# A two-layer cached-attention decode step: caches laid out with 64 consecutive keys in a partition, V loaded in pairs of slots

## The chip, the cores and the metric

The kernel runs on one core of a Trainium2 chip. The metric is device microseconds of one execution, lower is better. The core has five engines with a queue each: PE (TensorE, matrix products; its weight loads are a row of their own, PEld), DVE (VectorE), ACT (ScalarE), POOL (GpSimd) and SP (SyncE, which here only issues transfers). Sixteen DMA engines move data between the chip's main memory and the on-chip buffer of 128 partitions.

## The reference

One decode step for 8 batch rows, through an attention block A and an MLP block B, twice, with the same weights and the same caches both times. Everything is bfloat16.

```python
B, Sq, D = 8, 1, 512
Hq, Hkv, Sk, Dh = 32, 8, 8192, 128
...
q = (x @ wq)                      # 32 query heads of 128
k, v = repeat(k_cache, 4), repeat(v_cache, 4)      # 4 query heads share one cached head
p = softmax(q . k * Dh ** -0.5)
o = (p . v) @ wo
...
x = x + A(layernorm(x)); x = x + silu(layernorm(x) @ w1) @ w2
x = x + A(layernorm(x)); x = x + silu(layernorm(x) @ w1) @ w2
```

K and V hold 8 rows x 8 heads x 8192 keys x 128 values each, 128 MiB apiece. For one row and head that is 2 MiB of K and 2 MiB of V. Since a softmax and the sum over its keys don't depend on the order of the keys, any order will do as long as K and V agree on it.

## The kernel before

**Tasks.** A task is one layer, one batch row and one cached head (128 tasks). `make_tasks` (L141) writes out their order by hand. Heads 0, 1 and 2 of each row, and half of head 3, have their K loaded in both layers; the last 18 granules of K of each row (half of head 3, and heads 4 to 7) are *kept*: loaded for layer 0 and left in the buffer until layer 1 of the same row. For each row the order is: layer 0 of the heads 3 to 7 ("kept heads, first pass"), then five or six tasks that fill the time (heads 0 to 2 of other rows, of either layer), then layer 1 of heads 3 to 7 (little K to load, V only). The next row's first pass follows directly. While the filling tasks run, the row's own chain (output projection, LayerNorm, MLP, LayerNorm, query projection of layer 1) is worked off in small stages between them, since layer 1 needs its query.

**Granules, groups and slots.** A task's 8192 keys are four granules of 2048 keys (512 KB of K and of V), and each granule is two groups of 1024 keys. `ARENA` (L248) is 27 slots of one granule, 4 KB in each partition. In a granule, partition p holds 16 consecutive keys, and a granule is one solid 512 KB piece of memory (L354).

**Order of the loads.** `plan_loads` (L172) lists every load with the group before which it is needed and the group after which its slot is free again: a K granule is needed LT = 2 groups before its first group's scores and free after its second group's; a V granule is needed, and freed, LP = 12 groups behind its scores. The list is sorted by need, and each load takes the slot that comes free earliest. `issue` (L352) sends one load on SP, which first waits until the slot's last readers are done; `issue_until(p)` (L394) sends, after group p has been emitted, those at the head of the list whose slot is free by the plan. The list is never overtaken. At the start the first four K granules go out, then wq, then all loads into untouched slots, then wo, w1 and w2 (`load_rest`, L401).

**A group's work.** The main loop (L748) steps through the groups p, 1024 keys each:

- `emit_t` (L424): eight 128x128 transposes of K on PE into PSUM (L433), and a copy of 128x1024 back over the slot (by DVE, L441, or ACT, L439); kept K in layer 1 is already transposed.
- `emit_s` (L458): the scores of a granule, four matmuls of 512 columns (L464).
- the softmax of the task before, spread over the eight steps of the next (the table `soft`, L735): at step 0 the row maximum and a spread of it along the diagonal (`softmax_max`, `spread`, L475 and L477); at step 1 a matmul with a matrix of ones that hands it to all partitions (L485), the shift (`own`, `shift`, L488 and L491) and the exponential into `P` (ACT, L495); at step 3 the sums (L501, and on POOL L504); at step 4 the transposes of P (L513) and their copy to `PT` (L517); at step 7 the reciprocal (L524).
- `emit_pv` (L526): P times V, 12 groups behind the scores, 16 matmuls for a granule (L537), and at the task's end `emit_norm` (L542).

Buffers: two `PT`, separate `spread` and `own`, four sets of sums (NST = 4), a 128x128 matrix `ones`, a `far` of 64 columns (four equal copies of 16), and separate buffers for the LayerNorm (`xc`, `sq`, `xnT`, `vr`) and the MLP (`eh`, `hsT`). `op` (L320) adds the waits: an instruction waits for the last writer of what it reads, and for the readers of what it writes.

Of the kernel before, what the change touches and what calls it, by code (L numbers as in the profile page):

```python
# [5 lines left out]
HQ = 32  # L6
DH = 128
SM_SCALE = DH ** -0.5
LN_EPS = 1e-5
# [6 lines left out]
NSLOT = 27  # L16
KEEP = 18
LT = 2
PRE = 10
LP = 12  # L20
# [4 lines left out]
NPT = 2  # L25
NQB = 2
NST = 4
# [102 lines left out]
class Load:  # L130


    __slots__ = ("kind", "b", "g", "k", "need", "free", "slot", "after")

    def __init__(self, kind, b, g, k, need, free):
        self.kind, self.b, self.g, self.k = kind, b, g, k
        self.need, self.free = need, free
        self.slot, self.after = None, None
# [32 lines left out]

def plan_loads(tasks, kept, nslot, ngran):  # L172

    at = {t: i for i, t in enumerate(tasks)}
    loads = []
    for i, (layer, b, g) in enumerate(tasks):
        for k in range(ngran):
            i0 = i * GPT + k * GPG
            if layer == 0 or (g, k) not in kept:
                need = -1 if i0 < PRE else i0 - LT  # L180
                last = i if layer or (g, k) not in kept else at[(1, b, g)]
                loads.append(Load("K", b, g, k, need, last * GPT + (k + 1) * GPG - 1))
            loads.append(Load("V", b, g, k, i0 + GPG - 1 + LP, i0 + GPG - 1 + LP))
    loads.sort(key=lambda d: (d.need, d.kind))
    free = [(-2, s) for s in range(nslot)]
    for d in loads:
        free.sort()
        d.after, d.slot = free.pop(0)
        assert d.after < d.need or d.need == -1 and d.after == -2, (d.kind, d.need, d.after)
        free.append((d.free, d.slot))  # L190
    return loads
# [18 lines left out]
def _build(ctx, nc, A_x, A_k_cache, A_v_cache, A_wq, A_wo, B_w1, B_w2, out):  # L210
# [59 lines left out]
    QB = [sb([128, NGRAN - 1 + QUAD], BF16, "QB") for _ in range(NQB)]  # L270
    at1 = [sb([128, HQ], BF16, "at1") for _ in range(3)]
    at2 = sb([128, HQ, B], BF16, "at2")
    vr = sb([128, B], FP32, "vr")
    yr = sb([128, B], FP32, "yr")
    tr = sb([128, B], FP32, "tr")
    s1 = sb([128, B], FP32, "s1")
    s1a = sb([128, B], FP32, "s1a")
    xc = sb([128, KT, B], FP32, "xc")
    sq = sb([128, KT, B], FP32, "sq")
    xnT = sb([128, KT, B], BF16, "xnT")  # L280
    eh = sb([128, FT * B], FP32, "eh")
    hsT = sb([128, FT * B], BF16, "hsT")
# [3 lines left out]
    PT = [sb([128, CPB, NQ * USED], BF16, "PT") for _ in range(NPT)]  # L286
    ones = sb([128, 128], FP32, "ones")
    hm = sb([128, REP], FP32, "hm")
    real = sb([128, 1], FP32, "real")
    far = sb([128, NQ * USED], FP32, "far")  # L290
    rowmax = sb([128, 1], FP32, "rowmax")
    spread = sb([128, NQ * USED], FP32, "spread")
    own = sb([128, NQ * USED], FP32, "own")
    shift = sb([128, 1], FP32, "shift")
    rs = [sb([128, 1], FP32, "rs") for _ in range(NST)]
    ssm = [sb([128, REP], FP32, "ssm") for _ in range(NST)]
    ssa = [sb([128, REP], FP32, "ssa") for _ in range(NST)]
    rcp = [sb([128, REP], FP32, "rcp") for _ in range(NST)]

# [52 lines left out]
    def issue(d):  # L352
        cache = A_k_cache if d.kind == "K" else A_v_cache
        src = cache[d.b, d.g].rearrange("(k p c) d -> k p (c d)", k=NGRAN, p=128)[d.k]  # L354
        dst = ARENA[:, d.slot * SLOT:(d.slot + 1) * SLOT]
        dma(sp, dst, src, slsem[d.slot], writes=[r_half(d.slot, 0), r_half(d.slot, 1)])
        (k_slot if d.kind == "K" else v_slot)[(d.b, d.g, d.k)] = d.slot

    with nc.Block() as block:

        @block.sync
        def _(sync_eng):
# [11 lines left out]
            op(dve, lambda: dve.memset(ones[:, :], 1.0), writes=["ones"])  # L374
            for n in range(NQB):
                op(pool, lambda n=n: pool.memset(QB[n][:, :], 0.0), writes=[f"QB{n}"])
# [4 lines left out]
                    hm[:, :], lanes.rearrange("p c (r k) -> p r c k", k=NGRAN), AX.XY, ALU.add),  # L381
                reads=["ident"], writes=["hm"],
            )
            op(dve, lambda: dve.tensor_reduce(real[:, :], hm[:, :], AX.X, ALU.add), reads=["hm"], writes=["real"])
            for c in range(NQ):
                op(dve, lambda c=c: dve.tensor_scalar(
                    far[:, c * USED:(c + 1) * USED].rearrange("p (r k) -> p r k", k=NGRAN),
                    hm[:, :].unsqueeze(2).to_broadcast([128, REP, NGRAN]), real[:, 0:1], -FAR,
                    op0=ALU.subtract, op1=ALU.mult),
                   reads=["hm", "real"], writes=["far"])  # L390
# [15 lines left out]
            for _n in range(NGRAN):  # L406
                issue(queue.pop(0))
# [65 lines left out]
            def softmax_max(ti):  # L473
                bank = ti % NSCP
                op(dve, lambda: dve.tensor_reduce(rowmax[:, :], SCp[bank][:, :], AX.X, ALU.max),  # L475
                   reads=[f"SC{bank}"], writes=["rowmax"])
                op(dve, lambda: dve.tensor_scalar(  # L477
                    spread[:, :].rearrange("p (c q) -> p c q", q=USED), lanes, rowmax[:, 0:1], -SM_SCALE,
                    op0=ALU.mult, op1=ALU.mult),
                   reads=["ident", "rowmax"], writes=["spread"])  # L480

            def softmax_shift(ti):
                ob = ti % 2
                every = OTp[ob][:, 0:NQ * USED]
                mm_group([lambda: pe.matmul(every, ones[:, :], spread[:, :], start=True, stop=True)],  # L485
                         reads=["ones", "spread"], writes=[f"OT{ob}"])

                op(dve, lambda: dve.scalar_tensor_tensor(  # L488
                    own[:, :], every, real[:, 0:1], far[:, :], op0=ALU.mult, op1=ALU.add),
                   reads=[f"OT{ob}", "real", "far"], writes=["own"])  # L490
                op(dve, lambda: dve.tensor_reduce(shift[:, :], own[:, :], AX.X, ALU.min), reads=["own"], writes=["shift"])  # L491

            def softmax_exp(ti):
                bank, st = ti % NSCP, ti % NST
                op(act, lambda: act.activation(  # L495
                    P[:, :], SCp[bank][:, :], ACT.Exp, bias=shift[:, 0:1], scale=SM_SCALE, accum_out=rs[st][:, :]),
                   reads=[f"SC{bank}", "shift"], writes=["P", f"rs{st}"])

            def softmax_sum(ti):
                st = ti % NST  # L500
                op(dve, lambda: dve.tensor_scalar(  # L501
                    ssm[st][:, :], hm[:, :], rs[st][:, 0:1], None, op0=ALU.mult),
                   reads=["hm", f"rs{st}"], writes=[f"ssm{st}"])
                op(pool, lambda: pool.partition_all_reduce(ssa[st][:, :], ssm[st][:, :], 128, bass.bass_isa.ReduceOp.add),  # L504
                   reads=[f"ssm{st}"], writes=[f"ssa{st}"])

            def emit_pt(ti):
                pb = ti % NPT
# [9 lines left out]
                    PT[pb][:, :, :].rearrange("p x (c q) -> p x c q", q=USED),  # L518
                    tpv.rearrange("p x (c q) -> p x c q", q=QUAD)[:, :, :, 0:USED]),
                   reads=[f"TP{tb}"], writes=[f"PT{pb}"])  # L520

            def softmax_rcp(ti):
                st = ti % NST
                op(dve, lambda: dve.reciprocal(rcp[st][:, :], ssa[st][:, :]), reads=[f"ssa{st}"], writes=[f"rcp{st}"])  # L524

            def emit_pv(i):  # L526
# [3 lines left out]
                ob, pb = ti % 2, ti % NPT  # L530
                pv = PT[pb][:, :, :].rearrange("p x (c r k) -> p x c k r", c=NQ, k=NGRAN)
# [10 lines left out]
                mm_group(steps, reads=[r_half(slot, h), f"PT{pb}"], writes=[f"OT{ob}"])  # L542

            def emit_norm(ti):
# [6 lines left out]
                op(dve, lambda: dve.tensor_tensor(dst, OTp[ob][:, 0:REP * PVN:PVN], rcp[st][:, :], ALU.mult),  # L551
                   reads=[f"OT{ob}", f"rcp{st}"], writes=[rd])

            def ln_stages(xv, rx, n):

                xcv, sqv, xnv = xc[:, :, 0:n], sq[:, :, 0:n], xnT[:, :, 0:n]
# [7 lines left out]
                def second():  # L564
# [6 lines left out]
                        reads=["s1a", rx], writes=["xc"],  # L571
                    )
                    op(dve, lambda: dve.tensor_tensor(sqv, xcv, xcv, ALU.mult), reads=["xc"], writes=["sq"])
                    op(dve, lambda: dve.tensor_reduce(s1[:, 0:n], sqv.rearrange("p k b -> p b k"), AX.X, ALU.add),
                       reads=["sq"], writes=["s1"])
                    op(pool, lambda: pool.partition_all_reduce(s1a[:, 0:n], s1[:, 0:n], 128, bass.bass_isa.ReduceOp.add),
                       reads=["s1"], writes=["s1a"])
                def third():
                    v, y = vr[:, 0:n], yr[:, 0:n]
                    vi, yi = v.bitcast(INT32), y.bitcast(INT32)  # L580
                    op(dve, lambda: dve.tensor_scalar(v, s1a[:, 0:n], 1.0 / D, LN_EPS, op0=ALU.mult, op1=ALU.add),
                       reads=["s1a"], writes=["vr"])
                    op(dve, lambda: dve.tensor_scalar(yi, vi, 1, None, op0=ALU.logical_shift_right),
                       reads=["vr"], writes=["yr"])
# [4 lines left out]
                def newton(rounds):  # L589
                    v, y, t = vr[:, 0:n], yr[:, 0:n], tr[:, 0:n]  # L590
                    for _n in range(rounds):
                        op(dve, lambda: dve.tensor_tensor(t, y, y, ALU.mult), reads=["yr"], writes=["tr"])
                        op(dve, lambda: dve.scalar_tensor_tensor(t, t, -0.5, v, op0=ALU.mult, op1=ALU.mult),  # L593
                           reads=["tr", "vr"], writes=["tr"])
# [3 lines left out]
                def fourth():  # L598
# [3 lines left out]
                       reads=["xc", "yr"], writes=["xnT"])  # L602
# [51 lines left out]
            def block_stages(xs, rxs, n, fine=False):  # L654
# [4 lines left out]

                def expo():  # L660
                    op(act, lambda: act.activation(eh[:, 0:FT * n], MISC[:, 0:FT * n], ACT.Exp, scale=-1.0),
                       reads=["MISC"], writes=["eh"])

                def silu():
                    ev = eh[:, 0:FT * n]
                    op(dve, lambda: dve.tensor_scalar(ev, ev, 1.0, None, op0=ALU.add), reads=["eh"], writes=["eh"])
                    op(dve, lambda: dve.reciprocal(ev, ev), reads=["eh"], writes=["eh"])
                    op(dve, lambda: dve.tensor_tensor(hsT[:, 0:FT * n], MISC[:, 0:FT * n], ev, ALU.mult),
# [169 lines left out]
```

## Time and profile before

| | |
|---|---|
| time, median of 3 runs | 1208.69 us (1207.76 to 1209.6) |
| profiled execution: span from first to last instruction | 1205.7 us |
| bytes read from memory | 473.44 MB, 393 GB/s over the span |
| K loads, V loads | 368 and 512, 512 KB each |
| transposes of K on PE (L433) | 5888, 418.5 us busy |
| P times V on PE (L537) | 8192, 296.0 us busy |
| copies of transposed K: DVE (L441), ACT (L439) | 317.1 us, 278.7 us busy |
| mean granted TensorE clock | 0.977 |

The profile is of one execution, and its span is 3.0 us under the median of the three runs. Its rows give an engine's busy time, its share of the span and the count of its instructions. The rows in 40 slices show how the busy share, the clock and the transfer rate run over the span. "DMA packets" are the single pieces that the DMA engines move, counted by size. A group's idle time names what ended it, so a PE that waits for K shows it as released by the transfer. A window's line gives each engine's busy time in that stretch, the granted PE clock, the mean busy share of the 16 DMA engines (packets overlap, so it can be a little over 1), and GB/s.

### The profile page before, as it was taken

What the parts mean: (1) busy time and instruction counts of PE and PEld (TensorE: products, weight loads), DVE (VectorE), ACT (ScalarE), POOL (GpSimd) and SP (SyncE); (2) the same over time, 40 slices, a digit from 0 to 9 for tenths busy, and PEclk for the clock granted to TensorE, in tenths of its full rate; (3) what the DMA queues carried; (4) which work ended last, traced back from release to release, by engine and by line L of the source; (5) the groups of instructions that cost most, each with busy time, mean ns of one, the idle gap of its engine ahead of it and who ended that gap; (6) DMA issues with size and microseconds to landing.
All of it is one profiled execution on the core that took longest, in us unless ns stands there. A gap on an engine that the chain in (4) does not pass through costs nothing.

```text
span 1205.7 us, 45853 instructions
## 1 busy us (share of the span) xinstructions
PE 981.2 (81%) x20216; PEld 772.2 (64%) x20216; DVE 611.8 (51%) x1853; ACT 386.1 (32%) x670; POOL 70.8 (6%) x172
## 2 busy tenths in 40 slices
PE   2868898778888788878888898788888898889885
PEld 2656675667666676667666676667666675667564
DVE  2534564446445554546454554446454554456443
ACT  1323332333233332333233332333233333333231
POOL 0000000000000000000000000000000000000000
PEclk7889999999999999999999999999999999999996
DMA  9999999999999999999999999999999999999994
GB/s 370 385 398 408 403 405 406 408 406 399 396 408 408 408 371 404 408 407 403 399 408 407 405 378 408 409 407 395 385 408 407 401 402 407 408 404 398 390 408 172
DMA packets 133926, 476.43 MB, mean 395 GB/s; under 512 B 14160, under 2 KB 20064, under 8 KB 133216
## 3 DMA queue, kind: packets, MB, share of 16 engines
q1 hardware_dynamic: 133728, 473.51, 99.6%
q8 instruction: 159, 2.61, 0.9%
q14 instruction: 39, 0.32, 0.1%
HBM read 473.44 MB, written 0.01 MB: 393 GB/s over the span
## 4 chain that ended last, share of the span: by engine, by line
DMA 47%; PE 32%; DVE 11%; issue 5%; SPq 3%; ACT 2%; POOL 0%; POOLq 0%; ACTq 0%; DVEq 0%
DMA arena<-in_A_k_cache_dram 45%; PE TPp L433 9%; PE OTp L537 9%; PE SCp L464 5%; PE MISC L613 5%; DVE arena L441 3%; SPq L334 3%; DMA arena<-in_A_v_cache_dram 2%; ACT P L495 2%; PE OTp L485 2%; PE TPp L513 1%; DVE rowmax L475 1%; DVE PT L517 1%; PE MISC L631 1%; DVE tr L593 1%
## 5 line engine op out<-in xcount | busy, mean ns | idle before, releaser
L441 DVE COPY arena<-TPp 128x1024 bf16<-128x1024 bf16 x460 | 317.1, 690 | 384.0 <-PE TPp L433 383.6
L433 PE MATMUL TPp<-ident,arena 128*128 128x128 bf16 x5888 | 418.5, 221 | 110.4 <-DMA arena<-in_A_k_cache_dram 92.0
L433 PEld LDWEIGHTS TPp<-ident,arena 128*128 128x128 bf16 x5888 | 341.3, 99 | 129.7 <-DMA arena<-in_A_k_cache_dram 108.9
L439 ACT COPY arena<-TPp 128x1024 bf16<-128x1024 bf16 x276 | 278.7, 1010 | 395.5 <-PE TPp L433 395.4
L537 PEld LDWEIGHTS OTp<-PT,arena 128*128 128x128 bf16 x8192 | 243.1, 96 | 158.7 <-issue 104.5
L537 PE MATMUL OTp<-PT,arena 128*128 128x48 bf16 x8192 | 296.0, 184 | 33.3 <-DVE at L551 9.6
L464 PE MATMUL SCp<-arena,QB 128*32 128x512 bf16 x2048 | 206.8, 394 | 4.9 <-issue 2.1
L495 ACT ACTIVATE P<-SCp,shift 128x512 bf16<-128x512 f32 x128 | 88.0, 687 | 381.7 <-DVE shift L491 261.9
L504 POOL PARTITION_ALL_REDUCE ssa<-ssm x128 | 56.2, 439 | 940.8 <-DVE ssm L501 923.4
L475 DVE TENSOR_REDUCE rowmax<-SCp 128x1 f32<-128x512 f32 x128 | 87.5, 684 | 33.8 <-PE SCp L464 33.8
L464 PEld LDWEIGHTS SCp<-arena,QB 128*32 128x32 bf16 x2048 | 52.9, 93 | 53.0 <-issue 3.3
L485 PE MATMUL OTp<-spread,ones 128*128 128x64 f32 x256 | 55.2, 297 | 28.4 <-DVE spread L477 27.1
L513 PE MATMUL TPp<-ident,P 128*128 128x128 bf16 x512 | 50.0, 220 | 21.9 <-ACT P L495 20.2
L488 DVE SCALAR_TENSOR_TENSOR own<-OTp,real,far 128x64 f32<-128x64 f32 x128 | 36.3, 284 | 53.4 <-PE OTp L485 53.2
L485 PEld LDWEIGHTS OTp<-spread,ones 128*128 128x128 f32 x256 | 38.6, 190 | 36.9 <-DVE spread L477 35.5
L501 DVE TENSOR_SCALAR ssm<-hm,rs 128x4 f32<-128x4 f32 x128 | 28.8, 225 | 42.8 <-ACT P L495 42.8
L513 PEld LDWEIGHTS TPp<-ident,P 128*128 128x128 bf16 x512 | 32.0, 98 | 26.8 <-ACT P L495 23.8
L613 PE MATMUL MISC<-xnT,wq 128*128 128x32 bf16 (+1 forms) x1152 | 38.7, 176 | 4.2 <-issue 2.8
L517 DVE COPY PT<-TPp 128x256 bf16<-128x256 bf16 x128 | 36.4, 285 | 9.6 <-PE TPp L513 9.6
L631 PE MATMUL MISC<-at,wo 128*128 128x32 bf16 (+1 forms) x1152 | 39.9, 175 | 0.3 <-DVE at L551 0.3
L613 PEld LDWEIGHTS MISC<-xnT,wq 128*128 128x128 bf16 x1152 | 35.0, 96 | 5.3 <-issue 3.2
L631 PEld LDWEIGHTS MISC<-at,wo 128*128 128x128 bf16 x1152 | 35.3, 97 | 0.4 <-DVE at L551 0.4
(47 smaller groups left out, 296.3 us busy)
## 6 DMA issues: line engine op xcount, KB each, us to landing
arena<-in_A_v_cache_dram SPq DMA_DIRECT2D x512, 512.0 KB, 10.7
arena<-in_A_k_cache_dram SPq DMA_DIRECT2D x368, 512.0 KB, 15.1
wq<-in_A_wq_dram SPq DMA_DIRECT2D x1, 4096.0 KB, 16.3
wo<-in_A_wo_dram SPq DMA_DIRECT2D x1, 4096.0 KB, 26.5
w<-in_B_w_dram SPq DMA_DIRECT2D x2, 1792.0 KB, 23.1
P<-in_A_x_dram SPq DMA_DIRECT2D x1, 8.0 KB
out_dram<-P SPq DMA_DIRECT2D x1, 8.0 KB
```

The costliest lines, as they stand in the source:

```text
L433: lambda c=c: pe.transpose(tpv[:, c, :], chunk(slot, h * GRP + c), ident[:, :])
L439: op(act, lambda: act.copy(dst, TPp[tb][:, :]), reads=[f"TP{tb}"], writes=[r_half(slot, h)])
L441: op(dve, lambda: dve.tensor_copy(dst, TPp[tb][:, :]), reads=[f"TP{tb}"], writes=[r_half(slot, h)])
L464: lambda c=c: pe.matmul(SCp[bank][c * QUAD:(c + 1) * QUAD, :], QB[qn][:, NGRAN - 1 - k:NGRAN - 1 - k + QUAD], ARENA[:, slot * SLOT + c * K ...
L475: op(dve, lambda: dve.tensor_reduce(rowmax[:, :], SCp[bank][:, :], AX.X, ALU.max), reads=[f"SC{bank}"], writes=["rowmax"])
L485: mm_group([lambda: pe.matmul(every, ones[:, :], spread[:, :], start=True, stop=True)], reads=["ones", "spread"], writes=[f"OT{ob}"])
L495: op(act, lambda: act.activation(P[:, :], SCp[bank][:, :], ACT.Exp, bias=shift[:, 0:1], scale=SM_SCALE, accum_out=rs[st][:, :]), reads=[f" ...
L504: op(pool, lambda: pool.partition_all_reduce(ssa[st][:, :], ssm[st][:, :], 128, bass.bass_isa.ReduceOp.add), reads=[f"ssm{st}"], writes=[f ...
L513: lambda c=c: pe.transpose(tpv[:, c, :], P[:, c * 128:(c + 1) * 128], ident[:, :])
L537: lambda c=c, cc=cc: pe.matmul(otp, chunk(slot, h * GRP + c), pv[:, cc % CPB, cc // CPB % NQ, k, :].unsqueeze(2).to_broadcast([128, REP, P ...
L613: lambda o=o, k=k: pe.matmul(MISC[:, o * n:o * n + w], w_sb[:, k, o * 128:(o + 1) * 128], rhs_of(k).to_broadcast([128, w]) if n == 1 else ...
L631: lambda o=o, h=h: pe.matmul(MISC[:, o * w:(o + 1) * w], wo_sb[:, h, o * 128:(o + 1) * 128], rhs_of(h).to_broadcast([128, w]) if n == 1 el ...
```

## The change

**Layout.** A head's 8192 keys are now split over the partitions first: partition p holds keys 64p to 64p+63, 16 KB that lie together in memory. Granule k is the k-th quarter of that in every partition, 4 KB, and granules k and k+1 of a partition are one run of 8 KB.

**Wider loads.** A load may cover several granules that go to neighbouring slots: two for V (VWIDE), all the kept granules of a head for K (four, or two for head 3), one for other K (KWIDE). Only the semaphore of the first of its slots counts it. A wide load is needed when its first granule is, and it can go out when the last of its slots is free.

**Plan.** There are 28 slots. The upper 18 are homes, a fixed place for each kept granule; the other 10 are for streaming. Other loads may use a home too, if they are done with it at least AHEAD = 10 us before the kept head needs it. The plan keeps a clock (PACE: 1.24 us a group, 0.64 us where K is already there). For each load, in order of need, it takes the slot or run of slots with the longest lead (capped at ENOUGH = 14 us), then the least idle waiting of one slot for another, then the one that came free last. A load of two or four whose lead would be under EARLIEST (7 or 14 us) is split in halves.

**Small buffers.** To make room for the slot: one `PT`; `spread` and `own` lie in P's bytes, as do the MLP's buffers for all rows at once, while the LayerNorm's for all rows lie in PT's; two sets of sums; `ones` is a column that is repeated by the access pattern, `far` 16 columns repeated likewise; the rest are columns of one tensor `small`, and the chain's `xc`, `sq` and `eh` share columns and one name for the waits; `vr` is written over `s1a`.

```diff
-NSLOT = 27
+NSLOT = 28
...
+KWIDE = 1
+VWIDE = 2
+EARLIEST = {1: 0.0, 2: 7.0, 4: 14.0}
+ENOUGH = 14.0
+AHEAD = 10.0
+PACE = (1.24, 0.64)
...
-NPT = 2
-NST = 4
+NST = 2
...
 def plan_loads(tasks, kept, nslot, ngran):
...
+        if kind == "K":
+            need = -1 if i0 < PRE else i0 - LT
+            end = i if home is None else at[(1, b, g)]
+            free = [end * GPT + (k + 1) * GPG - 1 for k in ks]
+        else:
+            need = i0 + GPG - 1 + LP
+            free = [i * GPT + (k + 1) * GPG - 1 + LP for k in ks]
+        heapq.heappush(heap, (need, kind, i, ks, Load(kind, i, b, g, ks, need, free, home)))
...
+            for slot in range(nslot - n + 1):
+                held = free[slot:slot + n]
+                if any(r and lead(r[0], f) < AHEAD for r, f in zip(reserved[slot:slot + n], d.free)):
+                    continue
+                after = max(held)
+                waste = sum(clock[max(0, after)] - clock[max(0, f)] for f in held)
+                key = (-min(lead(d.need, after), ENOUGH), waste, -after, slot)
+                best = key if best is None else min(best, key)
+            if n > 1 and (best is None or -best[0] < EARLIEST[n]):
+                push(d.kind, d.task, d.ks[:n // 2])
+                push(d.kind, d.task, d.ks[n // 2:])
+                continue
+            d.slot = best[-1]
+        d.after = max(free[d.slot:d.slot + n])
...
-    PT = [sb([128, CPB, NQ * USED], BF16, "PT") for _ in range(NPT)]
-    ones = sb([128, 128], FP32, "ones")
+    PTb = sb([128, CPB * NQ * USED], BF16, "PT")
+    Pf = P[:, :].bitcast(FP32)
+    spread = Pf[:, 0:NQ * USED]
+    own = Pf[:, NQ * USED:2 * NQ * USED]
...
     def issue(d):
         cache = A_k_cache if d.kind == "K" else A_v_cache
-        src = cache[d.b, d.g].rearrange("(k p c) d -> k p (c d)", k=NGRAN, p=128)[d.k]
-        dst = ARENA[:, d.slot * SLOT:(d.slot + 1) * SLOT]
+        n = len(d.ks)
+        rows = cache[d.b, d.g].rearrange("(p c) d -> p (c d)", p=128)
+        src = rows[:, d.ks[0] * SLOT:(d.ks[0] + n) * SLOT]
+        dst = ARENA[:, d.slot * SLOT:(d.slot + n) * SLOT]
...
-            for _n in range(NGRAN):
+            while len(k_slot) < NGRAN:
                 issue(queue.pop(0))
...
-                mm_group([lambda: pe.matmul(every, ones[:, :], spread[:, :], start=True, stop=True)],
-                         reads=["ones", "spread"], writes=[f"OT{ob}"])
+                mm_group([lambda: pe.matmul(every, ones.to_broadcast([128, 128]), spread, start=True, stop=True)],
+                         reads=["ones", "P"], writes=[f"OT{ob}"])
```

## The prediction

> **What bounds the kernel now.** I read the page from the top (span, engines, slices, queues), then windows of the DMA rate, then what the PE waits for. First the page:
>
> ```profile
> span 1205.7 us, 45853 instructions
> PE 981.2 (81%) x20216; PEld 772.2 (64%) x20216; DVE 611.8 (51%) x1853; ACT 386.1 (32%) x670; POOL 70.8 (6%) x172
> ...
> GB/s 370 385 398 408 403 405 406 408 406 399 396 408 408 408 371 404 408 407 403 399 408 407 405 378 408 409 407 395 385 408 407 401 402 407 408 404 398 390 408 172
> DMA packets 133926, 476.43 MB, mean 395 GB/s; under 512 B 14160, under 2 KB 20064, under 8 KB 133216
> ...
> q1 hardware_dynamic: 133728, 473.51, 99.6%
> ...
> arena<-in_A_v_cache_dram SPq DMA_DIRECT2D x512, 512.0 KB, 10.7
> arena<-in_A_k_cache_dram SPq DMA_DIRECT2D x368, 512.0 KB, 15.1
> ```
>
> The queue of the loads is at 99.6% of 16 engines, no other engine is over 81%, and 880 cache loads of 512 KB are 461 of the 473 MB. The rate has a lid of 408 GB/s. Cut into fifty windows of 24 us, 34 stand at 402 GB/s or more: in 68% of the time the transfers are the bound. In the rest (around 430, 560, 700 and 850 us) the LayerNorm, MLP and query chain of a batch row runs beside the attention, and the rate falls. Seven windows, each line giving busy us (and counts) of PE, PEld, DVE, ACT, POOL, then PE clock, DMA share and GB/s:
>
> ```profile
> 8.00:18.00 10.00, 2.92 (x28) 2.66 (x28) 1.61 (x8) 1.01 (x1) 0.43 (x3) 0.93 1.01 419
> 10.00:14.00 4.00, 2.73 (x26) 2.46 (x24) 1.34 (x7) 1.01 (x1) 0.00 (x0) 1.00 1.02 430
> 18.00:48.00 30.00, 19.91 (x331) 16.36 (x332) 13.27 (x36) 7.14 (x11) 1.28 (x3) 0.68 1.02 408
> 48.00:60.00 12.00, 11.01 (x216) 8.63 (x214) 8.37 (x21) 4.79 (x9) 0.43 (x1) 1.00 1.09 351
> 240.00:264.00 24.00, 19.33 (x373) 15.39 (x374) 11.77 (x30) 9.29 (x15) 1.29 (x3) 1.00 1.03 408
> 432.00:444.00 12.00, 11.27 (x274) 9.63 (x272) 8.11 (x30) 3.81 (x6) 0.99 (x3) 1.00 1.01 389
> 444.00:456.00 12.00, 9.74 (x187) 6.75 (x187) 5.24 (x15) 3.09 (x6) 0.44 (x1) 0.90 0.98 360
> ```
>
> DMA share is full in all seven, but the rate differs by what moves. By bytes, 2.1 to 6.3 MB into the stream (8 to 18 us) is wq, whose rows are 8 KB: 419, in its middle 430. From 18 us come cache loads of 4 KB a partition: 408. From 48 us comes wo, 1 KB rows: 351. So the lid belongs to the packet: 16 engines at 408 take 160.6 ns for 4 KB, at 351 46.7 ns for 1 KB; a straight line through both has 8.7 ns at zero bytes and gives 419 for 8 KB and 425 for 16 KB. An 8 KB row is indeed one packet: 710 packets are not under 8 KB, wq's 512 and 198 of the two instruction queues. In 240:264 the PE idles 4.7 of 24 us and waits 3.8 of them for K:
>
> ```profile
> PE TPp L433 <- DMA arena<-in_A_k_cache_dram: 3.8, 6, 0.7
> ```
>
> So it could run 16% faster there; in 432:444 it is busy 11.3 of 12 us, and a faster transfer buys nothing.
>
> **The change, part by part.** Bytes stay the same; everything below is against the profiled execution, 1205.7 us of span. The median of the three runs, 1208.7, is 3.0 above it, and I add that.
>
> *V in pairs.* 512 granules are 268.4 MB: 657.9 us at 408. Rate for 8 KB packets: between 419 and 430. I take 427, nearer the upper, since the 10 us window has 4 KB loads at its two ends: 628.7 us, 29.3 saved if all counts. Only the share of time in which transfers bind counts: 0.68, so 19.9. Not every pair stays a pair: the planner splits one that would be issued less than 7.0 us ahead. In slot-groups per full task of 8 groups: before, 9 streaming slots give 72, of which a K slot holds its data 3 groups (4 x 3 = 12), so 60 are left for 8 granules, 7.5 groups each. After, 10 slots give 80, minus 12, minus 8 (in each pair the first half waits 2 groups for the second to come free, and the second lies landed 2 groups longer), again 60. 7.5 groups at the plan's own 1.24 us is 9.3 us, over the threshold, but neighbours must come free together; I take 0.9 paired (bounds 0.6 and 1). **17.9 us saved** (bounds 7.0, with 419 and 0.6, and 22.9, with 430 and 1).
>
> *Kept K, one load a head.* 18 granules in 8 rows are 75.5 MB, 185.0 us at 408. The trace has no timed 16 KB transfer; bounds are no gain over 408 and 430, and I take 427 as for V: 176.8. They are loaded in the stretches where transfers bind (the kept heads' first pass and the layer-1 pass ahead of it, both at 408). **8.2 us saved** (0 to 9.5). The first granule now lands with the fourth, 3 x 1.28 = 3.8 us later; its home comes free in the layer-1 pass of the row before, five tasks ahead, so this is covered. Without cover it would be 40 loads x 3.8, 154 us.
>
> *The other K.* 224 granules stay 4 KB packets, but 16 KB apart instead of one solid 512 KB. Zero; bounds in the rivals.
>
> *Issues on SP.* 880 become about 550. SP is in order, so a wide load whose second slot is still read holds all loads behind it, about 2 groups or 2.6 us. Behind it the queue has 10.7 (V) to 15.1 us (K) from issue to landing, so it does not run dry: zero. Fewer issues (0.3 us each at least) save nothing either, for the same reason.
>
> *Start.* The plan now prefers the slot last freed that leaves 14 us. Followed by hand, eight K granules and one V pair get untouched slots; the next K (task 2) reuses slot 0, so the first batch stops at ten slots instead of 27, and wo, w1 and w2 go out ahead of it. Queued are then 2.1 + 4.2 + 3.1 + 7.9 = 17.3 MB, good until some 45 us; the first scores are done at 35 us (34.7 in the trace), which frees slot 0. Zero; if the queue emptied, at most the 11 us between 35 and 46.
>
> *Packed buffers.* PT is single: its copy (step 4 of the task after next) follows the last group of values that read the old one (step 3) and precedes the new one's first reader (step 5); the copy waits for transposes behind those values in PE's own order. Spread and own lie in P: written at step 0, P's last reader was step 4 of the task before, some 5 us earlier. Sums with two buffers instead of four: reader eight steps earlier. LayerNorm's and the MLP's shared buffers are used in turn by one serial chain. All zero; uncovered, it would be a PT copy and its wait (0.29 + 0.69 us) in the chain stretches, 0.32 x 128 x 0.98 = 40 us. Three DVE operations fewer at the start (234 ns each) lie beside the wait for wq: zero. The ones weights are now one column repeated: a load of 189 ns, 256 of them; a repeated moving operand runs at 175 ns in wo like any other, so zero; doubled, 256 x 0.189 x 0.32 = 15.5 us.
>
> *Tail.* The last V load is a pair, so the end has two granules' values behind the last landing instead of one, and a granule's 16 matmuls took 0.82 us there: **+0.8**.
>
> Sum: 17.9 + 8.2 - 0.8 = 25.3. 1205.7 - 25.3 + 3.0 = **1183.4 us**. What is late next: the PE's own pace in the chain stretches, which grow from 32% of the time.
>
> **The rivals.**
> *More.* 430 for both, all V paired, half of the slower windows gain too (they hold K and V at 380 to 400, not far under the lid): 33.7 x 0.84 + 9.5 - 0.8 = 37.0, so 1171.7. For it: 430 stood four us; against: 432:444.
>
> *Less.* The fixed cost per packet is the line's 8.7 ns or under, so 8 and 16 KB both run at 419, and 0.6 is paired: 17.3 x 0.68 x 0.6 + 4.9 - 0.8 = 11.1, so 1197.6. For it: the 10 us mean is 419. The Trainium skill (DMA: Bandwidth & Descriptors, "Why small descriptors are slow (HBM only)") speaks for it more sharply: about 3 cycles per packet beside one for each 32 bytes, an estimate of 1.1% from 4 to 8 KB and 1.7% to 16 KB, which would leave about 1202; the trace's step from 408 to at least 419, 2.7%, is more than that.
>
> *Nothing.* wq's 430 was an effect of an empty chip, and packets do not matter: 1209. Against it: 18:48 is as early and shows 408.
>
> *Slower, pairs run the queue dry.* Each of some 230 wide loads waits at SP for its second slot until engines idle. The gain is gone at 25.3 / 230 = 0.11 us of idle each; at 0.25 it is 57 us, 1241. For it: SP is in order and loads are small in number, ten slots. Against: no binding window has a DMA share under 1, and the backlog is four times the 2.6 us.
>
> *Slower, the pitch.* If K at 4 KB every 16 KB fell to the 351 of the 1 KB rows, 334.5 instead of 287.8 us x 0.68 = 31.8, so 1215; it decides at 376 GB/s. Against it: wq's partitions read pieces 1 MB apart at 419 and more. The same page ("Latency and other measured facts") has copies slow down with row pitches of 2 MiB and over; 16 KB is not among its pitches, and no row here shows one.
>
> **How the numbers follow.** Forecast (1176 to 1191) 0.48; more 0.18; less (up to 1206) 0.18; nothing 0.04; dry queue 0.07; pitch 0.05. 0.2%, 2.4 us, is about what this kernel's runs tell from no change. Faster 0.84, same 0.04, slower 0.12. From 1166 (430 for both, all of V paired, transfers binding throughout: 33.7 + 9.5 - 0.8 = 42.4) to 1206, leaving out the last three cases and the edge of "more".
>
> **What would show it.** Right: some 70,000 cache packets instead of 112,640; binding windows at 417 or more where full tasks run, 425 in the layer-1 passes; PE's 3.8 us of waiting per 24 us falling by a third or more. Wrong: binding windows still at 408 (packets), a DMA share under 1 there (dry queue), K windows under 408 (pitch), V issues well over 290 (splits), or new waits of DVE on P or PT. The prediction fails most simply if the lid at 8 KB is not what wq showed.

## The result and the profile after

The changed kernel takes 1225.26 us (median of 4 runs, 1219.49 to 1230.09) against 1208.22 us (4 runs) before: a ratio of 1.0142, 95% interval 1.0121 to 1.0162. It is slower; I had forecast 1183.4 us and faster. The profiled execution has a span of 1228.4 us (its own time is 1230.09). These lines of its page answer those shown of before:

```profile
span 1228.4 us, 45116 instructions
PE 1002.1 (82%) x20216; PEld 790.9 (64%) x20216; DVE 611.7 (50%) x1850; ACT 387.3 (32%) x670; POOL 70.5 (6%) x172
...
GB/s 357 386 425 406 376 394 423 423 370 376 397 421 417 366 350 418 423 394 384 408 424 387 365 372 422 420 336 344 392 426 406 374 378 422 419 368 378 378 415 173
DMA packets 82082, 476.37 MB, mean 388 GB/s; under 512 B 8400, under 2 KB 14304, under 8 KB 43488
...
q1 hardware_dynamic: 81888, 473.48, 96.6%
...
arena<-in_A_v_cache_dram SPq DMA_DIRECT2D x256, 1024.0 KB, 10.5
arena<-in_A_k_cache_dram SPq DMA_DIRECT2D x224, 512.0 KB, 8.9
arena<-in_A_k_cache_dram SPq DMA_DIRECT2D x32, 2048.0 KB, 14.6
arena<-in_A_k_cache_dram SPq DMA_DIRECT2D x8, 1024.0 KB, 15.1
```

The wide packets do what they should: slices that stood at the lid of 408 now stand at 417 to 426, and in 240:264 the PE waits 1.8 us for K instead of 3.8. But fourteen slices behind the first are at 336 to 378, where before only two were that low (371 and 378), and the queue's share of 16 engines is down from 99.6% to 96.6%. All 256 V loads are pairs; the plan split none.

Three stretches, before and after, as windows (busy us of PE, PEld, DVE, ACT, POOL; PE clock, DMA share, GB/s). First before:

```profile
200.00:240.00 40.00, 31.48 (x600) 24.30 (x595) 19.06 (x49) 14.32 (x23) 1.73 (x4) 1.00 1.03 408
262.00:272.00 10.00, 7.94 (x150) 6.14 (x148) 5.02 (x13) 3.81 (x6) 0.43 (x1) 1.00 1.03 401
290.00:312.00 22.00, 19.45 (x471) 16.38 (x471) 13.23 (x48) 6.72 (x10) 1.63 (x4) 1.00 1.01 388
```

and after:

```profile
200.00:240.00 40.00, 31.98 (x576) 24.96 (x577) 17.82 (x47) 12.31 (x20) 1.72 (x4) 0.91 1.01 422
262.00:272.00 10.00, 9.29 (x183) 7.24 (x180) 6.75 (x16) 4.82 (x7) 0.43 (x1) 1.00 0.83 300
290.00:312.00 22.00, 21.45 (x514) 18.41 (x510) 12.84 (x47) 7.90 (x13) 1.63 (x4) 0.92 0.96 361
```

In 200:240, a first pass of kept heads, the rate is 422 instead of 408. In 262:272, where the filling tasks' loads begin, the DMA share is 0.83 instead of 1.03: part of the time the engines have nothing to move. How much the queue holds is read from the time between issue and landing. The loads issued in 290:312 before (count, size, median us to landing):

```profile
arena<-in_A_v_cache_dram SPq DMA_DIRECT2D x10, 512.0 KB, 7.9
arena<-in_A_k_cache_dram SPq DMA_DIRECT2D x6, 512.0 KB, 7.6
```

and after:

```profile
arena<-in_A_v_cache_dram SPq DMA_DIRECT2D x5, 1024.0 KB, 6.6
arena<-in_A_k_cache_dram SPq DMA_DIRECT2D x6, 512.0 KB, 7.6
```

The page's medians over the whole run, 10.7 and 15.1 us before, hide that. In 200:240 a load of before lands after 16 us, in the filling tasks after about 8, and the fastest landing anywhere in its trace is 3.8. A pair of a megabyte that lands after 6.6 us has little ahead of it, since the fastest pair in the trace takes 5.1. Cut into steps of 1 us, the rate in the filling tasks behind the start is under 330 GB/s in 13 of 480 steps before and in 123 of 487 after.

To see where the time went I took, for each task, the time from one task's exponential on ACT to the next task's, and summed it by kind of task (one profiled execution each):

| us (in brackets GB/s) | start (7) | filling tasks (45) | first pass of kept heads (35) | layer-1 pass of kept heads (40) |
|---|---|---|---|---|
| before | 75.9 | 483.0 (397) | 361.3 (408) | 222.5 (405) |
| after | 77.9 | 492.3 (367) | 368.3 (415) | 229.4 (417) |
| pairs at 10 us of lead (below) | 78.2 | 466.6 (396) | 365.6 (418) | 222.5 (412) |

The start is kept apart because the changed order of its loads only shifts time there: tasks 1 and 2 take 9 us more and the first pass behind them 7 us less. Behind it the loss is 9 us in the filling tasks, 7 in the first passes and 7 in the layer-1 passes. The bytes show where it comes from. The filling tasks move 180.5 MB instead of 191.6, though they take longer, and the other two stages have to load what is missing there, at rates over those of before. In the filling tasks the PE waits 26.8 us for V instead of 2.7.

### The profile page after: what moved, and what is told of

Same layout as the page of the kernel before. It is cut to its first block, busy times and chain, and to the rows that moved or that the text cites. A ratio compares the mean times of both kernels' runs of the same rounds, so it can differ in the third digit from the quotient of the medians.

```text
span 1228.4 us, 45116 instructions
## 1 busy us (share of the span) xinstructions
PE 1002.1 (82%) x20216; PEld 790.9 (64%) x20216; DVE 611.7 (50%) x1850; ACT 387.3 (32%) x670; POOL 70.5 (6%) x172
## 3 DMA queue, kind: packets, MB, share of 16 engines
q1 hardware_dynamic: 81888, 473.48, 96.6%
## 5 line engine op out<-in xcount | busy, mean ns | idle before, releaser
L512 PEld LDWEIGHTS TPp<-ident,arena 128*128 128x128 bf16 x5888 | 364.2, 102 | 107.9 <-DMA arena<-in_A_k_cache_dram 84.5
L576 ACT ACTIVATE P<-SCp,small 128x512 bf16<-128x512 f32 x128 | 87.9, 687 | 371.3 <-DVE small L572 207.5
L584 POOL PARTITION_ALL_REDUCE small<-small x128 | 56.0, 437 | 957.0 <-DVE small L582 939.4
L554 DVE TENSOR_REDUCE small<-SCp 128x1 f32<-128x512 f32 x128 | 87.5, 684 | 38.1 <-PE SCp L543 38.1
L567 DVE SCALAR_TENSOR_TENSOR P<-OTp,small 128x64 f32<-128x64 f32 x128 | 36.3, 284 | 69.0 <-PE OTp L564 68.5
L564 PE MATMUL OTp<-P,small 128*128 128x64 f32 x256 | 54.8, 296 | 18.9 <-DVE P L556 16.7
L564 PEld LDWEIGHTS OTp<-P,small 128*128 128x128 f32 x256 | 38.8, 191 | 24.9 <-DVE P L556 23.1
L582 DVE TENSOR_SCALAR small<-small 128x4 f32<-128x4 f32 x128 | 28.8, 225 | 41.7 <-ACT P L576 41.7
L693 PE MATMUL MISC<-small,wq 128*128 128x32 bf16 x1024 | 35.2, 177 | 2.8 <-issue 1.5
L556 DVE TENSOR_SCALAR P<-ident,small 128x64 f32<-128x64 bf16 x128 | 32.6, 254 | 4.5
## 6 DMA issues: line engine op xcount, KB each, us to landing
arena<-in_A_k_cache_dram SPq DMA_DIRECT2D x8, 1024.0 KB, 15.1
```

The source lines that it names most:

```text
L512: lambda c=c: pe.transpose(tpv[:, c, :], chunk(slot, h * GRP + c), ident[:, :])
L554: op(dve, lambda: dve.tensor_reduce(rowmax, SCp[bank][:, :], AX.X, ALU.max), reads=[f"SC{bank}"], writes=["rowmax"])
L564: mm_group([lambda: pe.matmul(every, ones.to_broadcast([128, 128]), spread, start=True, stop=True)], reads=["ones", "P"], writes=[f"OT{ob}"])
L576: op(act, lambda: act.activation(P[:, :], SCp[bank][:, :], ACT.Exp, bias=shift, scale=SM_SCALE, accum_out=rs[st]), reads=[f"SC{bank}", "sh ...
L584: op(pool, lambda: pool.partition_all_reduce(ssa[st], ssm[st], 128, bass.bass_isa.ReduceOp.add), reads=[f"ssm{st}"], writes=[f"ssa{st}"])
```

## The experiments

A *lead* below is the number of groups between the group after which a load may be sent and the group before which it is needed, counted in the plan, in the order of the list (a load can't overtake the one ahead of it). Each ratio is against runs of the kernel before on the same chip.

**1. The layout alone**, in the kernel before.

```diff
-        src = cache[d.b, d.g].rearrange("(k p c) d -> k p (c d)", k=NGRAN, p=128)[d.k]
+        src = cache[d.b, d.g].rearrange("(p c) d -> p (c d)", p=128)[:, d.k * SLOT:(d.k + 1) * SLOT]
```

> The kernel before with only the new layout: every load is still one granule, 4 KB in each partition, but the pieces now lie 16 KB apart. If the pitch is what makes the changed kernel slower, this one is slower too: at 376 GB/s or less in the stretches where transfers bind, and 1225 us or more. If the pitch is harmless, it is within 0.2% of the kernel before (1206 to 1211 us), with 408 GB/s in those stretches.

1214.97 us, ratio 1.0064 (1.0044 to 1.0083): between the two expectations, a cost of some 7 us. It is not a lower lid. Before:

```profile
2.00:8.00 6.00, 0.00 (x0) 0.00 (x0) 0.00 (x0) 1.28 (x1) 0.00 (x0) 1.00 0.95 329
200.00:240.00 40.00, 31.48 (x600) 24.30 (x595) 19.06 (x49) 14.32 (x23) 1.73 (x4) 1.00 1.03 408
420.00:456.00 36.00, 30.39 (x706) 24.70 (x707) 20.01 (x67) 10.45 (x19) 2.10 (x5) 0.97 0.99 373
```

and with the new layout:

```profile
2.00:8.00 6.00, 0.00 (x0) 0.00 (x0) 0.00 (x0) 1.28 (x1) 0.00 (x0) 1.00 0.88 309
200.00:240.00 40.00, 31.98 (x604) 24.53 (x600) 19.10 (x50) 14.11 (x23) 1.73 (x4) 1.00 1.03 407
420.00:456.00 36.00, 29.38 (x658) 24.38 (x658) 20.60 (x73) 10.68 (x17) 2.13 (x5) 0.95 0.94 348
```

Where the queue is long, 407 against 408; in the filling tasks, where it is short, 348 against 373. The start (first line) is slower until 4 us and faster after that: the fourth K load lands 9.3 us after the span's start, against 9.5 before. Over all filling tasks behind the start the two traces take the same time, 482.7 and 483.0 us, but the new layout moves 188.8 MB in it instead of 191.6, 391 GB/s instead of 397. The missing 2.8 MB are 6.9 us at 408 GB/s, and the first and layer-1 passes, where transfers bind, take 5.2 and 2.2 us longer. The loss arises in one stage and shows in another.

**2. V one slot at a time**, in the changed kernel.

```diff
-VWIDE = 2
+VWIDE = 1
```

> The changed kernel with V loaded one slot at a time (VWIDE 1); the kept heads' wide K loads, the homes, the plan's choice of slots and the packed buffers stay. If the pairs are what lets the transfer queue run dry, it comes back to the kernel before or under it: 1195 to 1212 us, DMA share 1.0 in the filling tasks, at 408 GB/s. If the homes and the plan's preference for the slot freed last are the cause, or the packed buffers, it stays at 1218 us or more, with the DMA share under 1 in the same places.

1203.66 us, ratio 0.9966 (0.9949 to 0.9983). The pairs account for all of the loss, and for more: without them the rest of the change is a small gain.

**3 and 4. The packed buffers, and the slot.** The changed kernel with the old `plan_loads`, one granule a load, with 27 and with 28 slots.

```diff
-    heap = []
...
+    loads.sort(key=lambda d: (d.need, d.kind))
+    free = [(-2, s) for s in range(nslot)]
+    for d in loads:
+        free.sort()
+        d.after, d.slot = free.pop(0)
```

> The changed kernel's packed buffers and layout, with the kernel before's plan, one granule a load, 27 slots. It differs from the layout-only kernel by the packed buffers alone. If single PT, spread and own inside P, two sets of sums and the repeated column of ones cost anything, it shows here: 1215 us or more, with DVE waits on P and PT. If they cost nothing, it is within 0.3% of the layout-only kernel.

> As the run before, with 28 slots: ten streaming slots of one granule. The extra slot adds one granule (1.28 us at 408 GB/s) to the backlog. If the backlog is what keeps the rate at its lid beside the chain, it gains 1 to 6 us over 27 slots; if the PE sets the pace there, it gains under 2 us.

27 slots: 1214.02 us, ratio 1.0062 (1.0045 to 1.0079), the same as the layout alone, so the packed buffers cost nothing. 28 slots: 1210.63 us, 1.0027 (1.0013 to 1.0042): the slot is worth 3.4 us.

**5. Each pair sent as two loads**, in the pair's slots and at its place in the list.

```diff
+        if d.kind == "V":
+            for m, k in enumerate(d.ks):
+                e = Load("V", d.task, d.b, d.g, (k,), d.need, d.free[m:m + 1], None)
+                e.slot, e.after = d.slot + m, free[d.slot + m]
+                loads.append(e)
+        else:
+            loads.append(d)
...
-        loads.append(d)
```

> The changed kernel with its plan and its slots for the pairs, but each pair sent as two loads of one granule, one behind the other in the list: the first half goes when its own slot is free, and each half counts on its own semaphore. V's packets are 4 KB again. If what starves the queue is the wait of a pair for its second slot (and that its data count only when both halves are there), it comes back to the run with single V, 1200 to 1208 us. If it is the slots that the plan picks, it stays at 1218 us or more.

1220.29 us, ratio 1.0100 (1.0083 to 1.0117). Against run 2, which has the same 4 KB packets, 16.6 of the changed kernel's 21.6 us of loss stay with the halves apart. So the larger part is the slots that pairs are given and their place in the list, and with these when a load can go. The other 5 us, and whatever the wide packets gain in the changed kernel, are the price of sending and counting a pair whole.

What the PE waits for differs between the two. First run 2, then run 5:

```profile
PE TPp L512 <- DMA arena<-in_A_k_cache_dram: 77.4, 79, 3.5
PE OTp L616 <- DMA arena<-in_A_v_cache_dram: 8.8, 9, 4.4
```

```profile
PE TPp L518 <- DMA arena<-in_A_k_cache_dram: 93.9, 72, 6.7
PE OTp L622 <- DMA arena<-in_A_v_cache_dram: 2.5, 6, 0.7
```

With the halves apart, K is late, not V: 16.5 us more waiting, about the whole loss. Run 10 below has the same K leads and waits 78.5 us for K, so short K leads alone don't do it. The reading that fits is that a V load which can go late holds back the K loads behind it in the list.

**6. The longest lead instead of the slot freed last**, pairs as they are.

```diff
-ENOUGH = 14.0
+ENOUGH = 1e9
```

> The changed kernel with ENOUGH raised out of reach: a load takes the slot with the longest lead, not the one freed last among those with 14 us; pairs stay. Worked out from the plan, the pairs in the filling tasks are then sent 8.9 groups ahead instead of 8.0, and none of them stands behind a load whose slot comes free later. If the late choice starves the queue, it falls to 1212 us or less; if the pairs as such do, it stays within 6 us of the changed kernel (1219 to 1230).

1226.06 us, ratio 1.0146 (1.0131 to 1.0161), no change. The plan's late choice is not the cause. By the plan the shortest lead of a pair in the filling tasks stays at 6 groups, though the mean rises by 0.9.

**7 and 8. A pair only where it has 10 us**, without and with the raised ENOUGH.

```diff
-EARLIEST = {1: 0.0, 2: 7.0, 4: 14.0}
+EARLIEST = {1: 0.0, 2: 10.0, 4: 14.0}
```

> The changed kernel with the threshold under which a pair is split raised from 7 to 10 us. By the plan 149 of 256 V loads stay pairs, nearly all of them in the passes of the kept heads; in the filling tasks 25 of 93 do. If pairs are worth their 424 GB/s where the backlog is long and cost only where it is short, this beats the single-V kernel (1203.7) and the kernel before: 1190 to 1202 us. If pairs cost wherever they are, it lies between the single-V kernel and the changed one: 1205 to 1220.

> As the run before, and ENOUGH out of reach too, so that the plan sends every load as early as a slot allows. If the backlog is what counts, it is 1 to 6 us faster than with ENOUGH at 14; if the late choice costs nothing, it is the same within 2 us.

1194.15 us, ratio 0.9883 (0.9867 to 0.9899), and 1194.54 us, 0.9888 (0.9871 to 0.9906). One number in the changed kernel turns it from 1.4% slower into 1.2% faster than before. Run 7, with run 8 the same within its interval, is the fastest kernel of the study. The same windows of run 7:

```profile
200.00:240.00 40.00, 30.80 (x562) 24.26 (x558) 17.68 (x47) 13.43 (x22) 1.73 (x4) 0.91 1.02 423
262.00:272.00 10.00, 9.46 (x182) 7.45 (x177) 6.43 (x18) 4.55 (x7) 0.86 (x2) 1.00 1.00 374
290.00:312.00 22.00, 20.08 (x487) 17.04 (x484) 12.89 (x45) 7.84 (x12) 1.63 (x4) 1.00 1.01 390
```

The long-queue stretch keeps its 423; the two others come back to a DMA share of 1.00 and 1.01, though the first at 374 GB/s, not the 401 of before. Of the steps of 1 us in the filling tasks, 18 of 462 are under 330 GB/s.

**9. Short leads without pairs**: single V and 26 slots.

```diff
-NSLOT = 28
+NSLOT = 26
...
-VWIDE = 2
+VWIDE = 1
```

> The single-V kernel with 26 slots instead of 28, so eight for streaming; no pairs anywhere in V. By the plan, V in the filling tasks is then sent 7.3 groups ahead on average and 6 at the least, K 8.1 and 7 (with 28 slots: 9.2 and 8, 10.0 and 9; the changed kernel with pairs: 8.0 and 6, 9.2 and 7). If a short lead is the whole of what pairs do wrong, this kernel loses as much as they do: 1218 us or more against 1203.7. If pairs do something else (a lump of 1 MB, two halves that count together), it stays under 1212.

1221.72 us, ratio 1.0117 (1.0092 to 1.0141). Granule by granule, a plan whose V leads go down to 6 groups costs nearly what the pairs cost. K's leads fall with them here (8.1 groups on average and 7 at the least, instead of 10.0 and 9), and the PE waits 90.1 us for K instead of run 2's 77.4, so this run alone does not say which of the two it is. What the PE waited for V in all (us, times, longest): before, after, and this run have

```profile
PE OTp L537 <- DMA arena<-in_A_v_cache_dram: 8.1, 18, 1.0
```

```profile
PE OTp L616 <- DMA arena<-in_A_v_cache_dram: 33.5, 47, 2.3
```

```profile
PE OTp L616 <- DMA arena<-in_A_v_cache_dram: 16.9, 30, 4.6
```

**10. The pair's early place without its neighbouring slots**: single V, 28 slots, the second granule listed where its pair would be.

```diff
-VWIDE = 2
+VWIDE = 1
...
-            need = i0 + GPG - 1 + LP
+            need = i * GPT + ks[0] // 2 * 2 * GPG + GPG - 1 + LP
```

> The single-V kernel with 28 slots, but the second granule of each pair stands in the list where the pair would stand, two groups earlier, and takes any slot. It pays the pair's early place in the queue, without the need for two neighbouring slots. By the plan K is sent 9.2 groups ahead as with pairs, V 9.2. If the early place is the cost, 1215 us or more; if the neighbouring slots are (they cut V's lead to 6 groups at worst), it stays within 6 us of the single-V kernel: 1200 to 1210.

1205.60 us, ratio 0.9984 (0.9972 to 0.9997), 2 us more than run 2. The early place costs little. K's leads are those of the changed kernel here (9.2 groups, 7 at the least), V's stay at 8 or more. Runs 5, 9 and 10 together put most of the loss on V's shortest leads, which the search for two neighbouring slots cuts from 8 groups to 6 (in 66 of the pairs in the filling tasks). Run 6 had raised the mean lead and left the shortest, and gained nothing. How run 9's loss divides between V and K is not shown. The mean rate of the filling tasks goes with the times: 396 GB/s in run 7, 391 in run 2, 389 in run 10, 382 in run 9, 378 in run 5, 368 in run 6 and 367 in the changed kernel.

**11 and 12. 32 keys in a partition**: the layout in blocks of 1 MB, pieces 8 KB apart, in the kernel before (its edit is below) and in run 7's, where pairs and kept heads then come in pieces of 8 KB.

```diff
+        src = cache[d.b, d.g].rearrange("(j p c) d -> j p (c d)", j=2, p=128)[d.k // 2][:, d.k % 2 * SLOT:(d.k % 2 + 1) * SLOT]
```

> The kernel before with 32 consecutive keys in a partition: every load is a granule of 4 KB a partition at a pitch of 8 KB, half of a solid 1 MB. The 16 KB pitch cost 0.64%, 7.4 us. If the cost grows with the pitch, this one costs less: 1209 to 1213 us. If any gap between the pieces costs the same, 1214 to 1216 us.

> The kernel with the 10 us threshold (1194.2 us) on the layout of 32 consecutive keys: pairs are one solid megabyte in pieces of 8 KB, kept heads come in 8 KB pieces instead of 16 KB, single granules lie at a pitch of 8 KB. If the pitch of the single granules costs, it gains 2 to 5 us: 1189 to 1192. If 16 KB pieces are worth more than that, it loses up to 3 us.

1218.74 us, ratio 1.0095 (1.0069 to 1.0120), outside both expectations on the slow side, and 1198.51 us, 0.9925 (0.9902 to 0.9949), a little more lost than expected. The cost of the gaps does not shrink with the pitch (the intervals of runs 1 and 11 overlap). Run 12 gives a clean reading of 8 KB packets in a long queue, as 15.7 of the 16.76 MB in 200:240 are such:

```profile
200.00:240.00 40.00, 31.20 (x575) 24.37 (x571) 17.67 (x46) 12.46 (x21) 1.72 (x4) 0.91 1.01 419
```

**13. The threshold at 8.5 us**, and **14. kept K granule by granule**, the latter with 10 us.

```diff
-EARLIEST = {1: 0.0, 2: 7.0, 4: 14.0}
+EARLIEST = {1: 0.0, 2: 8.5, 4: 14.0}
```

```diff
-            push("K", i, ks, slot)
             for n in range(len(ks)):
-                reserved[slot + n].append(i * GPT + ks[0] * GPG - LT)
+                push("K", i, ks[n:n + 1], slot + n)
+                reserved[slot + n].append(i * GPT + ks[n] * GPG - LT)
```

> The changed kernel with the threshold for a pair at 8.5 us instead of 7 (10 in an earlier run). By the plan 181 of 256 V loads stay pairs: 72 of 80 in the layer-1 passes (41 with 10 us), 26 of 93 in the filling tasks (25 with 10 us). If it is the pairs in the filling tasks that cost, and the others pay, it is as fast as with 10 us or faster: 1189 to 1195. If pairs sent 8 groups ahead in the layer-1 passes cost too, it lies above 1198.

> The kernel with the 10 us threshold, but each kept granule of K is loaded by itself into its home, 4 KB a partition. The prediction priced the wide loads of kept K at 8.2 us. If that holds, this is 1200 to 1205; if the stretches in which they are loaded are not bound by transfers, it stays at 1194 to 1197.

1198.99 us, ratio 0.9924 (0.9901 to 0.9946), and 1199.10 us, 0.9939 (0.9920 to 0.9958). Run 13 has 32 more pairs, 31 of them in the layer-1 passes with leads of 8 groups or more (K's shortest lead falls from 9 to 7 groups with them), and loses 0.4%, as the second of its expectations had it: about 5 of the 31 us between run 7 and the changed kernel, so the rest lies with what 7 us admits and 8.5 us does not, 67 pairs in the filling tasks and 8 in the layer-1 passes. Run 14's time fell between its two expectations: wide loads of kept K are worth 0.0056 of 1208 us, 6.8 us (5.0 by the two medians).

## Why the prediction was wrong

**The step that failed** is "Issues on SP": "Behind it the queue has 10.7 (V) to 15.1 us (K) from issue to landing, so it does not run dry: zero." Those are medians over the whole run. In the filling tasks the same trace has 7.6 to 7.9 us (290:312; 8.2 over all of them), of which 3.8 is the least a load ever takes: some 4 us of cover, not 11. A tenth of the loads there land within 6.2 us, which leaves 2.4, less than the 2.6 that the prediction itself set against the cover. All of this stands in the trace of before. After the change the rate there is 367 GB/s instead of 397, and the pairs that go with too little lead, which this step put at nothing, cost 31 us (the changed kernel against run 7).

**The paragraph on pairs failed with it.** It worked out equal leads, 7.5 groups each before and after, from a count of slots, and saw that "neighbours must come free together". But it used that only to choose how many pairs the plan would split, and took the mean for what every load gets. The kernel feels the shortest lead (runs 6 and 7): 6 groups at the plan's 1.24 us are 7.4 us, and loads issued there take 6.6 to 7.6 us to land. The threshold of 7 us let all of them through (1.0 paired, not 0.9).

**The windows were priced on one side only.** I wrote that beside the chain "a faster transfer buys nothing", took 32% of the time out of the gain, and never asked what a later transfer costs there. That is where the transfers were lost. At 388 GB/s with a DMA share of 1.01 (290:312), those stretches were already below the lid of 408 as well as busy on PE. Two of the signs that the prediction named for being right did show (422 GB/s in 200:240, and 1.8 us of waiting for K in 240:264); they were to be looked for only in the stretches that gained.

**The rival "pairs run the queue dry"** had the right sign at a chance of 0.07, but looked for a low DMA share in the binding windows, where it stayed at 1.01 (200:240), and named only part of the mechanism: the wait at SP for the second slot. Run 5 shows that sending the halves apart takes 5 us off; the neighbours' shorter lead is the larger part.

**The pitch** was entered as zero, with a rival that lowered K's rate everywhere to 351. The layout costs 0.64%, 7.4 us, in another way: the lid stays, and short queues deliver less. That this rival's 1215 is also the time of run 1 is chance. (Its "decides at 376 GB/s" leaves out its own factor of 0.68; with it, it is 361.) The Trainium skill's rule (DMA: Bandwidth & Descriptors, "Latency and other measured facts") puts slow copies at row pitches of 2 MiB and more; the runs here show a cost at 16 KB and no smaller one at 8 KB. By which part of the memory, no run shows.

**The packet terms were right in kind, and a little high.** The straight line through the 1 KB and 4 KB rows gave 419 GB/s for 8 KB, and run 12 measures 419; I had taken 427, swayed by 430 in four microseconds of wq. The Trainium skill's count of about 3 cycles a packet (DMA: Bandwidth & Descriptors, "Why small descriptors are slow (HBM only)") would give an estimate of 1.1% from 4 to 8 KB; the measured step is 2.7%. Kept K: 8.2 us forecast, 5.0 to 6.8 measured (run 14). V: run 7 has 149 pairs, 156 MB, which is 382.9 us at 408 and 372.9 at 419, so 10.0 us; run 7 against run 2 is 9.5. That it shows nearly whole fits pairs that lie where transfers bind.

**Zero and zero:** the packed buffers (run 3 against run 1), single PT and spread inside P among them; the column of ones still loads in 191 ns. The start, forecast at zero, took 2 us more in all. The slot I had cancelled against the pairs' needs is worth 3.4 us by itself. Single effects add up to run 7: 7.4 - 3.4 - 6.8 - 9.5 = -12.3 us from 1208, 1196, against 1194 measured. The last two are themselves differences from run 7, so what this tests is run 2: 7.4 - 3.4 - 6.8 gives 1205, against 1203.7 measured. That leaves about nothing for the homes and the plan's choice of slots, which no run has by themselves. Putting the too-close pairs back adds 31.

Open: why gaps between pieces slow a short queue, and why the PE's clock falls more often. Its mean fell from 0.977 to 0.944 and the PE's busy time rose by 21 us for the same 20216 matmuls. But 17.5 of these lie in the first passes behind the start, where the PE still waits 46.7 us for K, and only 3.7 in the filling tasks; and run 7 at 0.958 is faster than before, run 9 at 0.960 slower. So the clock does not decide.

## What to carry to other kernels

Read the cover of a wait from the stretch in which the wait falls: issue to landing there, less the shortest landing in the trace, not the page's median. When buffers are planned ahead, look at the shortest lead of each kind of load, and ask of each merge of two buffers what it does to that. A wider transfer is worth its packet rate where the queue is long; where it is short, keep the loads small, which here was one threshold and 2.5% of the time.

## What the runs showed of the hardware

Reading 4 KB pieces at a pitch of 8 or 16 KB, instead of one solid 512 KB, leaves the rate of a full queue at 407 to 408 GB/s, but lowers the mean rate of the filling tasks, where the queue is short, from 397 GB/s to 391 and 393 (runs 1 and 3, 16 KB) and 392 (run 11, 8 KB), and costs 0.6% to 0.95% of the kernel. A transfer's rate in a full queue goes by its packets: 408 GB/s at 4 KB, 419 at 8 KB, 422 to 423 in a mix of 8 and 16 KB.
